# The way into attention made anew: maxima of the first heads turned into rows by TensorE, running sums put into K by VectorE, zero matmuls in early gaps

## The chip, the cores and the metric

The kernel runs on one core of one Trainium2 chip. The time is device microseconds of one execution. A core has TensorE (PE; its weight loads are listed as PEld), VectorE (DVE), ScalarE (ACT), GpSimd (POOL) and SyncE (SP, which issues nearly all DMAs here).

## What is computed

Attention for 4 batches of 8 heads, 576 positions of 64 dimensions, with a causal mask and a bias from running sums of s, and then two layers over 2304 tokens, each a product with a 512x2048 matrix, an activation and a product with a 2048x512 matrix.

```python
scores = q @ k.T / sqrt(64)
cum = cumsum(maximum(s, 0))                      # along the positions
bias = -(cum[:, None] - cum[None, :])
scores = where(causal, -1e9, scores + minimum(bias, 0))
attn = exp(scores - max(scores)); attn = attn / (sum(attn) + 1e-9)
x = attn @ v                                     # to (2304, 512)
h = x @ w_in;  x = (h - tanh(h)) @ w_out         # first layer
h = x @ w2_in; out = (h * clip(h + 3, 0, 6) / 6) @ w2_out
```

## The kernel before

**An order worked out ahead.** The kernel's functions only declare operations: `plan.op` with an engine, an estimated duration, the operations it comes after, the buffers it uses and a priority, and `plan.dma` the same for SyncE with a size. `Plan.schedule` then runs through them as a simulation, with estimated latencies (`LAT`, `DMA_US`), and the program is issued in the order of the starts that it finds. On the chip each engine goes through its own instructions in this order and waits at each for what it needs. Buffers are taken from pools; the six PSUM banks of the attention are one pool, and an operation that isn't `greedy` leaves two of them. Operations marked `port` use the SBUF port that DVE and POOL share; the planner doesn't let them overlap.

**A pair of heads.** `heads(p)` handles heads 2p and 2p+1; there are 16 pairs. q and k come as 64 rows of 576 columns a head. For products of high accuracy in a rounded type each operand is split in a high and a low part. The first pair of tiles (`firsts`, called Q and K) holds the high parts in rows 0 to 63 and four rows more: K has the running sum (high and low part, rows 64 and 65) and ones (66, 67); Q has ones (64, 65) and the negated maxima (66, 67). So the bias and the subtraction of the maximum come out of the same product. The second pair of tiles (also Q and K in the profile) holds the other combinations: `q2` copies Q's high part by DMA, `ql` and `kl` are POOL's subtractions (lines 427 and 437), `k2` a copy on ACT (433). `q1` (ACT, 421) and `kh` (DVE, 430) make the high parts of the first tiles.

**Maxima.** `mx` (line 481) multiplies the high parts for the maxima, in six matmuls a head, into `wide` and two banks; `rd` (490) reduces them on DVE with the causal mask into a column of maxima for each of five blocks of positions, `Mt`. Since the score product needs them as rows, `mf` negates and splits them (515, 516) and transposes them on DVE in blocks of 32 (519), `mo` writes them to DRAM (`mdram`) and `mi` reads them back into rows 66 and 67 of Q. Pair 0 does so head by head, the others for both heads at once.

**Scores and values.** `st` (575) makes the scores, transposed, in four chunks a head (15 matmuls, three of them the mask with an identity); `ex` (578) is the exponential on ACT, `pv` (605) the product with v in 14 matmuls, `ov` (628) the way out of PSUM.

**The start.** s is loaded for all 32 heads; DVE's `cum` clamps and scales it (371), forms running sums (372) and splits them (375, 376); a DMA puts head 0's two rows into K, and the rest goes through DRAM (`cdram`). Before it DVE fills the constant rows of head 0's Q and K and K's padding (341 to 343), and POOL those of the three other pairs of tiles, with masks and the identity.

**What comes behind.** While attention runs, twelve half blocks of the first layer's weights are read and rebuilt from two words each by ACT and DVE (`convert`, lines 748 to 779), ten more blocks afterwards. Then the first layer (830, 861) and the second (1122, 1198) follow, almost all matmuls.

Of the kernel before, what the change touches and what calls it, by code (L numbers as in the profile page):

```python
# [30 lines left out]
NW = 6  # L31
LATE_D = (7, 8, 11, 12)
# [28 lines left out]
PRIO = {  # L61
# [3 lines left out]
}  # L65
# [44 lines left out]
class Plan:  # L110
    LAT = {"PE": 0.30, "ACT": 0.05, "DVE": 0.09, "POOL": 0.09, "V": 0.0}
    DMA_US, DMA_KB_US, ISSUE = 1.6, 220.0, 0.55
# [26 lines left out]
    def schedule(self):  # L139
# [12 lines left out]
        while done < len(self.ops):  # L152
# [14 lines left out]
            while again:  # L167
                again = False
                for e in ready:
# [48 lines left out]
                    for n in o.next:  # L218
                        n.left -= 1
                        n.ready = max(n.ready, o.end)  # L220
# [18 lines left out]
def kernel(  # L239
# [87 lines left out]
    zeroed = [f32(m) for m in MTp.free] + [m.rearrange("p a i -> p (a i)") for m in mtp.free]  # L327
    s_t, c_t = (rb_t[0:NH, i * S : (i + 1) * S] for i in range(2))
    cp = [rb_t[0:NH, i * S : (i + 1) * S].bitcast(F32R) for i in (2, 3)]
# [8 lines left out]
    def prep_first(i):  # L338
        q1, k1 = firsts[i]
        eng = nc.gpsimd if i else nc.vector  # L340
        eng.memset(f32(q1)[64:68], 1.0)
        eng.memset(f32(k1)[64:68, :, 0:S], 1.0)
        eng.memset(f32(k1)[0:68, :, S:SP], 0.0)

    def prep_second():
        for _, k2 in seconds:
            nc.gpsimd.memset(f32(k2)[:, :, S:SP], 0.0)
# [17 lines left out]
    def prep_rest():  # L365
        for m in zeroed:
            nc.gpsimd.memset(m, 0.0)


    def cum():  # L370
        nc.vector.tensor_scalar(s_t, s_t, 0.0, 8.0, op0=ALU.max, op1=ALU.mult)
        nc.vector.tensor_tensor_scan(
            out=c_t, data0=c_t, data1=s_t, initial=0.0, op0=ALU.mult, op1=ALU.add
        )
        nc.vector.tensor_copy(cp[0], c_t)
        return nc.vector.tensor_sub(cp[1], c_t, f32(cp[0]))
# [944 lines left out]
```

## Time and profile before

| | |
|---|---|
| median of 3 runs | 959.87 us (958.36 to 960.94) |
| profiled execution | 957.06 us, span 955.3 us |
| mean granted TensorE clock | 0.999 |
| PE, DVE, ACT, POOL busy | 98%, 70%, 49%, 17% of the span |

The span reaches from the first to the last instruction of the profiled execution; its own time also holds what lies around it. A busy share is an average over stages with different limits. A group of instructions is named by its line, engine, operation and tiles (out<-in). In brackets behind an instruction stands how long its engine sat idle before it and what it then waited for. Matmuls overlap, so a busy PE can still run below its best rate.

### The profile page before, as it was taken

What the parts mean: (1) busy time and instruction counts of PE and PEld (TensorE: products, weight loads), DVE (VectorE), ACT (ScalarE), POOL (GpSimd) and SP (SyncE); (2) the same over time, 40 slices, a digit from 0 to 9 for tenths busy, and PEclk for the clock granted to TensorE, in tenths of its full rate; (3) what the DMA queues carried; (4) which work ended last, traced back from release to release, by engine and by line L of the source; (5) the groups of instructions that cost most, each with busy time, mean ns of one, the idle gap of its engine ahead of it and who ended that gap; (6) DMA issues with size and microseconds to landing.
All of it is one profiled execution on the core that took longest, in us unless ns stands there. A gap on an engine that the chain in (4) does not pass through costs nothing.

```text
span 955.3 us, 14956 instructions
## 1 busy us (share of the span) xinstructions
PE 933.0 (98%) x5560; PEld 831.9 (87%) x5560; DVE 672.8 (70%) x1107; ACT 464.9 (49%) x714; POOL 161.2 (17%) x106
## 2 busy tenths in 40 slices
PE   3999999999999999999999999999999999999998
PEld 3777777778878888998888888999999999999997
DVE  7887778789988766685676834657776577764763
ACT  2677677754534443444344333444454444544441
POOL 8344755600000000012222222000000000000000
PEclk9999999999999999999999999999999999999999
DMA  5667786796236448555546681776886767877672
GB/s 121 189 176 186 212 208 204 186 331 208 98 128 223 176 156 282 177 179 197 198 155 207 228 292 46 244 229 208 250 307 228 232 199 258 298 235 223 210 224 97
DMA packets 70521, 195.91 MB, mean 205 GB/s; under 512 B 11634, under 2 KB 20338, under 8 KB 69168
## 3 DMA queue, kind: packets, MB, share of 16 engines
q1 hardware_dynamic: 70448, 194.95, 64.3%
q8 instruction: 44, 0.72, 0.3%
q14 instruction: 29, 0.24, 0.1%
HBM read 143.75 MB, written 44.09 MB: 197 GB/s over the span
## 4 chain that ended last, share of the span: by engine, by line
PE 92%; DVE 3%; DMA 2%; ACT 1%; issue 1%; SPq 0%; DVEq 0%; ACTq 0%
PE bank L830 20%; PE bank L861 20%; PE pair L1198 19%; PE pair L1122 18%; PE bank L605 8%; PE bank L575 5%; DVE junk L490 1%; PE wide L481 1%; DMA tq<-in_q_dram 1%; PE bank L481 1%; DMA Q<-mdram 0%; DMA rdram<-rb 0%; ACT w L778 0%; DVE K L430 0%; DVE f_w L1142 0%
## 5 line engine op out<-in xcount | busy, mean ns | idle before, releaser
L861 PE MATMUL bank<-gg,w 128*128 128x512 f32 (+1 forms) x960 | 234.3, 368 | 0.5 <-ACT gg L849 0.3
L830 PE MATMUL bank<-xx,w 128*128 128x512 f32 (+1 forms) x960 | 233.2, 368 | 0.0
L861 PEld LDWEIGHTS bank<-gg,w 128*128 128x128 f32 x960 | 170.1, 189 | 30.9 <-ACT gg L849 1.3
L830 PEld LDWEIGHTS bank<-xx,w 128*128 128x128 f32 x960 | 170.5, 188 | 30.4
L1122 PE MATMUL pair<-op_w,w 128*128 128x384 f32 x648 | 118.0, 334 | 0.6 <-DVE f_w L1142 0.6
L841 ACT ACTIVATE g<-bank 128x512 f32<-128x512 f32 (+1 forms) x80 | 44.5, 556 | 148.2 <-PE bank L830 124.9
L1198 PE MATMUL pair<-w,op_W 128*128 128x256 f32 x918 | 115.1, 283 | 0.0
L1122 PEld LDWEIGHTS pair<-op_w,w 128*128 128x128 f32 x648 | 112.4, 188 | 1.2 <-DVE f_w L1142 0.9
L1198 PEld LDWEIGHTS pair<-w,op_W 128*128 128x128 f32 x918 | 112.8, 192 | 0.0
L605 PE MATMUL bank<-pt,vf 128*66 128x320 f32 (+4 forms) x448 | 106.9, 360 | 0.3 <-ACT pt L578 0.3
L851 POOL TENSOR_TENSOR gg<-g,gg 128x512 fp32r<-128x512 f32 x32 | 47.5, 1486 | 345.0 <-ACT gg L849 307.8
L845 DVE TENSOR_TENSOR g<-bank,g 128x512 f32<-128x512 f32 (+1 forms) x80 | 50.8, 635 | 64.4 <-ACT g L841 63.7
L575 PE MATMUL bank<-Q,K 128*128 128x320 f32 (+9 forms) x384 | 88.7, 352 | 1.6 <-ACT stage L628 1.1
L575 PEld LDWEIGHTS bank<-Q,K 128*128 128x128 f32 (+3 forms) x384 | 63.5, 186 | 23.3 <-ACT stage L628 1.7
L578 ACT ACTIVATE pt<-bank 128x512 f32<-128x512 f32 (+2 forms) x128 | 62.4, 500 | 33.3 <-PE bank L575 31.6
L849 ACT ACTIVATE gg<-g 128x512 fp32r<-128x512 f32 (+1 forms) x80 | 47.0, 587 | 43.4 <-DVE g L845 35.0
L490 DVE CUSTOM_DVE_ANT_0 junk<-bank,maskA 128x512 bf16<-128x512 f32 (+2 forms) x96 | 45.0, 469 | 20.6 <-PE bank L481 13.2
L605 PEld LDWEIGHTS bank<-pt,vf 128*66 128x66 f32 x448 | 50.5, 141 | 6.7 <-ACT pt L578 0.5
L427 POOL TENSOR_TENSOR Q<-tq,Q 64x1152 fp32r<-64x1152 f32 (+1 forms) x17 | 42.4, 2494 | 53.6 <-PE bank L575 9.0
L490 DVE CUSTOM_DVE_ANT_0 junk<-wide,maskA 128x384 bf16<-128x384 f32 x64 | 41.8, 653 | 10.0 <-PE wide L481 5.4
L437 POOL TENSOR_TENSOR K<-tq,K 64x1152 fp32r<-64x1152 f32 (+1 forms) x17 | 42.8, 2519 | 20.3 <-ACT stage L628 6.3
L1198 PE MATMUL pair<-w,op_B 128*128 128x256 f32 x342 | 44.1, 283 | 0.0
(305 smaller groups left out, 1303.3 us busy)
## 6 DMA issues: line engine op xcount, KB each, us to landing
w<-wdram SPq DMA_DIRECT2D x149, 512.0 KB
wdram<-cv SPq DMA_DIRECT2D x56, 512.0 KB
raw_c<-in_w_dram SPq DMA_DIRECT2D x11, 1024.0 KB
raw_b<-in_w_dram SPq DMA_DIRECT2D x11, 1024.0 KB
raw_a<-in_w_dram SPq DMA_DIRECT2D x12, 512.0 KB
vf<-in_v_dram SPq DMA_DIRECT2D x16, 330.0 KB
rb<-rdram SPq DMA_DIRECT2D x8, 576.0 KB
xdram<-xb SPq DMA_DIRECT2D x16, 288.0 KB
```

Source lines behind the costliest of these rows:

```text
L490: nc.vector.tensor_tensor_reduce(out=junk[0:rr, 0:w], in0=r(b)[0:rr, col : col + w], in1=maskA[0:rr, m0 : m0 + w], scale=1.0, scalar=-3.0e ...
L575: nc.tensor.matmul(o, w, x, start=(i == 0), stop=(i == len(mms) - 1), skip_group_check=True)
L578: nc.scalar.activation(r(pt), r(b)[:, 0 : CW[c]], AF.Exp, scale=0.125)
L605: nc.tensor.matmul(r(po[bank])[0:DV, oc : oc + n], r(vf)[:, j, hh, :], r(pts[c])[:, col : col + n], start=(j == 0), stop=(bank == 0 and c ...
L830: nc.tensor.matmul(r(ps)[:, 0:w], wt[:, c, :], x(c)[:, 0:w], start=(part == 0 and c == 0), stop=(part == 2 and c == NCC - 1),)
L841: nc.scalar.activation(r(g)[:, 0:w], r(ps)[:, 0:w], AF.Tanh)
L845: nc.vector.tensor_sub(x, r(ps)[:, 0:w], x)
L849: gho = plan.op("ACT", vec_us(w, 1.2, 205), lambda: nc.scalar.activation(r(gh)[:, 0:w], r(g)[:, 0:w], AF.Copy), [m, to_gg], [g, gh], base)
L851: glo = plan.op("DVE" if beside else "POOL", vec_us(w, 0.96, 155) if beside else vec_us(w, 0.44, 160), lambda: (nc.vector if beside else n ...
L861: nc.tensor.matmul(r(acc[e])[:, 0:w], a[:, es], bb[:, 0:w], start=f, stop=l)
L1122: nc.tensor.matmul(bank(k)[:, l], w[hw][:, l, kc], r(x)[:, hx, kc], start=(i in (1, 5, 2) and j == 0 and kc == 0), stop=(j == 2 and kc == ...
L1198: nc.tensor.matmul(r(c[k])[:, m * 256 : (m + 1) * 256], r(x)[:, hx, l, m * P : (m + 1) * P], w[hw][:, l], start=(i == order[chain_first[k] ...
```

## The change

Running sums: ACT clamps and scales s in place of DVE (`relu`). The sums now lie in partitions 64 to 96, with a copy of s for head 1 in partition 96 that ACT's own DMA queue loads, so that DVE can copy the high rows of heads 0 and 1 straight into K (`crow`); the low rows of these two follow by DMA. Head 0's and head 1's maxima are formed without the low row. For pair 0 ACT makes `kh`. Constant rows of pairs 1 to 3 come by DMA from those of pair 0 (`ones`), and the paddings of K are no longer filled; no product reads them.

Maxima of pairs 0 and 1 (`TURN`): instead of `mf`, `mo` and `mi` there is `turn`, twice a head (blocks 0 and 1, then 2 to 4). DVE writes the negated high and low parts beside two ones into four columns a block, PE multiplies each block by the identity, which gives four rows in PSUM, and ACT copies these into rows 64 to 67 of Q. The chunks of `mx` are taken in reverse order, so that blocks 0 and 1 are ready first, and the first chunk of scores waits only for them. The other pairs keep their way, with the negation as a subtraction from zeros and no `port` mark.

PE: ten matmuls of 512 columns on a tile of zeros at the start (`warm`), and ahead of head 1's scores zero matmuls of 256 columns wherever the planned order leaves a gap of over 0.2 us (`fill`, four fifths of the gap, 0.115 us each). They write to a bank that is held until then.

Order: all priorities are new; a table `EARLY` shifts those of the first six pairs one by one, and a table `first` orders the operations of the first six heads. Loads of q, k and v of the first pairs are tied to other operations. The planner's estimates of DMA and matmul durations change.

```diff
+TURN = (0, 1)
+WARM = 10
+EARLY = {...}
+LAG_Q = {3: 1, 4: 4, 5: 2}
+LAG_V = {1: 1, 2: 2, 3: 2, 4: 2}
+FILL_H = 1
-    DMA_US, DMA_KB_US, ISSUE = 1.6, 220.0, 0.55
+    DMA_US, DMA_KB_US, ISSUE = 1.9, 230.0, 0.62
...
-    return (4 * n / 2.4 + 6) / 1e3 if f32 else max(0.1, (n / 2.4 + (13 if n > 128 else 5)) / 1e3)
+    return (4 * n + 20) / 2.4e3 if f32 else (n + 32) / 2.4e3
...
-    s_t, c_t = (rb_t[0:NH, i * S : (i + 1) * S] for i in range(2))
+    s_t, c_t = (rb_t[D : D + NH + 1, i * S : (i + 1) * S] for i in range(2))
+    identr = att.tile([P, P], F32R, name="identr")
+    turn_t = att.tile([P, 2 * len(TURN), 5, 4], F32R, name="turn")
...
-        eng.memset(f32(k1)[0:68, :, S:SP], 0.0)
-            nc.gpsimd.memset(f32(k2)[:, :, S:SP], 0.0)
...
-        nc.vector.tensor_scalar(s_t, s_t, 0.0, 8.0, op0=ALU.max, op1=ALU.mult)
...
+    ls1 = plan.op("ACT", 0.62, lambda: nc.scalar.dma_start(s_t[NH : NH + 1], s[1:2]), prio=lead - 90, name="ls1")
+    pk0 = plan.op("POOL", 1.2, lambda: ones_k(0, nc.gpsimd), [pma], prio=lead - 39)
+    pq0 = plan.op("DVE", 1.15, lambda: ones_q(0, nc.vector), [pm0], prio=lead - 30.5)
+    sa = plan.op("ACT", 0.65, lambda: nc.scalar.activation(s_t, s_t, AF.Relu, scale=8.0), [ls, ls1], prio=lead - 30, name="relu")
+    cm = plan.op("DVE", 1.4, lambda: nc.vector.tensor_tensor_scan(
+        out=c_t, data0=c_t, data1=s_t, initial=0.0, op0=ALU.mult, op1=ALU.add), [sa, pq0], prio=lead - 29, name="cum")
+    cr = [plan.op("DVE", 0.46, lambda hh=hh: nc.vector.tensor_copy(c_row(hh, 0), c_t[NH * hh : NH * hh + 1]), [cm, pk0], prio=lead - 28 + 3 * hh, name="crow", port=True) for hh in range(2)]
...
+    cu1 = [plan.dma(lambda hh=hh: move(c_row(hh, 1), cp[1][hh : hh + 1]), 5, [cl, pk0], prio=lead - 24 + hh, name=f"cu0_lo{hh}") for hh in range(2)]
...
+    def warm():
+        for _ in range(WARM):
+            nc.tensor.matmul(r(wb)[:, 0:512], maskA[:, 0:P], maskA[:, 0:512], start=True, stop=True)
+    def fill(us):
+        for _ in range(int(us / 0.115)):
+            nc.tensor.matmul(r(wb)[:, 0:256], maskA[:, 0:P], maskA[:, 0:256], start=True, stop=True)
...
+        ones = firsts[0][1][66:68, :, 0:S]
+        def put(x):
+            move(firsts[p][x][64 + 2 * x : 66 + 2 * x, :, 0:S], ones)
+        return [plan.dma(lambda x=x: put(x), 9, [cl], prio=t, name=f"ones{p}") for x in range(2)]
...
+            def turn(hh, g):
+                i0, i1 = ((0, 2), (2, 5))[g]
...
+                    nc.vector.tensor_sub(slot[:, i0:i1, 2], none[:, 0 : i1 - i0], m)
+                    return nc.vector.scalar_tensor_tensor(
+                        out=slot[:, i0:i1, 3], in0=m, scalar=-1.0, in1=f32(slot)[:, i0:i1, 2], op0=ALU.mult, op1=ALU.subtract
+                    )
+                def rows():
+                    for i in range(i0, i1):
+                        nc.tensor.matmul(r(b)[0:4, (i - i0) * P : (i - i0 + 1) * P], slot[:, i], identr, start=(i == i0), stop=(i == i1 - 1), skip_group_check=True)
+                def put():
+                    nc.scalar.activation(r(b1)[0][64:68, hh, q0:q1], r(b)[0:4, 0 : q1 - q0], AF.Copy)
...
-            deps = [omi[x], oq2[x], ok2[x], oql[x], okl[x], pid]
+            low = [oq2[x], ok2[x], oql[x], okl[x], pmt] + (cu1 if p == 0 else [])
+            deps = [low + omi[hh][:1]] + [low + omi[hh]] * 3
...
+    filled = plan.op("V", 0.0, lambda: None, [wm, *st_done[FILL_H][:1]], [wb], prio=0, name="filled")
...
+        if o.eng == "PE":
+            if o.start < filled.start and gap and o.start - gap > 0.2:
+                fill(0.8 * (o.start - gap) - 0.1)
+            gap = o.start + o.dur
```

## Rows read from the trace of the kernel before

**Rows 1.** The page: PE's busy time, and its busy tenths in 40 slices.

```profile
PE 933.0 (98%) x5560; PEld 831.9 (87%) x5560; DVE 672.8 (70%) x1107; ACT 464.9 (49%) x714; POOL 161.2 (17%) x106
...
PE   3999999999999999999999999999999999999998
```

**Rows 2.** Windows: stretch, length, busy us per engine, granted clock, DMA share, GB/s.

```profile
0.00:20.00 20.00, 6.71 (x21) 5.32 (x21) 14.98 (x34) 6.33 (x7) 16.68 (x31) 1.00 0.42 102
20.00:40.00 20.00, 18.16 (x94) 13.71 (x93) 16.72 (x56) 10.82 (x19) 9.11 (x5) 1.00 0.70 196
60.00:100.00 40.00, 40.00 (x260) 31.68 (x259) 32.06 (x103) 30.19 (x58) 22.75 (x10) 1.00 0.73 184
20.00:200.00 180.00, 176.63 (x1110) 138.25 (x1110) 144.65 (x436) 128.32 (x244) 97.04 (x44) 1.00 0.75 197
```

**Rows 3.** Windows of line 481 alone, the maxima: PE and PEld busy.

```profile
0.00:50.00 50.00, 16.40 (x60) 11.73 (x60) 1.00 0.60 154
60.00:100.00 40.00, 9.94 (x42) 6.65 (x42) 1.00 0.73 184
```

**Rows 4.** Windows of line 575 alone, the scores: PE and PEld busy.

```profile
0.00:50.00 50.00, 11.91 (x60) 9.43 (x60) 1.00 0.60 154
60.00:100.00 40.00, 23.00 (x114) 16.50 (x115) 1.00 0.73 184
```

**Rows 5.** Timeline to the first matmul: start, us, engine, line, out<-in.

```profile
1.76 1.12 DVE L341 MEMSET Q<- 4x1280 f32 x1 [0.30 <-issue]
3.08 1.02 DVE L342 MEMSET K<- 4x1152 f32 x1 [0.19 <-issue]
...
3.96 0.68 ACT L421 ACTIVATE Q<-tq 64x576 fp32r<-64x576 f32 x1 [1.94 <-DMA tq<-in_q_dram]
...
4.25 1.12 DVE L371 TENSOR_SCALAR rb<-rb 32x576 f32<-32x576 f32 x1
5.40 1.35 DVE L372 TENSOR_TENSOR_SCAN rb<-rb 32x576 f32<-32x576 f32 x1
6.78 0.45 DVE L375 CAST rb<-rb 32x576 fp32r<-32x576 f32 x1
7.26 0.75 DVE L376 TENSOR_TENSOR rb<-rb 32x576 fp32r<-32x576 f32 x1
...
8.74 1.40 POOL L427 TENSOR_TENSOR Q<-tq,Q 64x576 fp32r<-64x576 f32 x1 [2.11 <-DVE K L430]
...
9.94 1.14 PE L481 MATMUL wide<-K,Q 66*128 66x384 f32 x3 [9.94 <-DMA K<-rb]
```

**Rows 6.** Timeline, 11 to 36 us: head 0's maxima, first scores, heads 2 and 3.

```profile
11.24 0.56 DVE L490 CUSTOM_DVE_ANT_0 junk<-wide,maskA 128x384 bf16<-128x384 f32 x1 [2.37 <-PE wide L481]
...
14.39 0.71 DVE L515 TENSOR_SCALAR MT<-Mt 128x5 fp32r<-128x5 f32 x1
...
15.57 1.13 DVE L430 CAST K<-tq 64x1152 fp32r<-64x1152 f32 x1
...
19.64 5.35 POOL L437 TENSOR_TENSOR K<-tq,K 64x576 fp32r<-64x576 f32 x3
...
22.40 0.63 PE L575 MATMUL bank<-Q,K 128*128 128x256 f32 x2
...
27.56 0.21 DVE L519 STREAM_TRANSPOSE mrow<-MT 128x32 f32<-128x32 f32 x1
...
29.31 0.38 ACT L628 ACTIVATE xb<-bank 66x256 f32<-66x256 f32 x1 [2.58 <-PE bank L605]
...
30.76 0.67 SPq L258 DMA_DIRECT2D Q<-mdram  x1
...
35.04 0.39 PE L575 MATMUL bank<-Q,K 68*128 68x256 f32 x1 [0.46 <-DMA Q<-mdram]
```

**Rows 7.** Timeline: the same three maxima matmuls (512, 256 and 128 columns), twice.

```profile
10.88 0.95 PE L481 MATMUL bank<-K,Q 66*128 66x512 f32 x3
...
28.36 0.57 PE L481 MATMUL bank<-K,Q 66*128 66x512 f32 x3
```

More of the change, by code (lines that the diff above doesn't have):

```diff
@@ L219, in schedule @@
                         n.left -= 1
-                        n.ready = max(n.ready, o.end)
+                        n.ready = max(n.ready, free[o.eng] if o.eng == n.eng != "SP" else o.end)
                         if n.left == 0:
@@ L503, in heads, with maxima @@
-        rd_done.extend(rds)
+            move(k1[64:66, :, 0:S], cdram[2 * p : 2 * p + 2].rearrange("a i s -> i a s"))
+        if p == 0:
+            ocu = [[cr[0]], [cr[1]]]
+        else:
+            ocu = [[plan.dma(cu, 5, [al, co], [b1], t0 + PRIO["cu"] + shift("cu"), name=f"cu{p}")]] * 2
         omi = []
-        for i, a in enumerate(parts):
+        def maxima(i, a):
             n = a.stop - a.start
@@ L538, in heads, with mx, rd @@
             first_mf.append(omf)
-            omi.append(plan.dma(mi, 5, [omo], [b1], u, name=f"mi{p}"))
-        lv = plan.dma(lambda: nc.sync.dma_start(r(vf).rearrange("p j a d -> p (j a d)"), v[p]), 338, first_mo[1:2] if p else first_mo[:1], [vf], t0 + PRIO["lv"], name=f"lv{p}")
+            omi.extend([[plan.dma(mi, 5, [omo], [b1], u, name=f"mi{p}")] * 2] * n)
+        mm_mx, mm_pe = {}, {}
+        for hh in range(2):
+            rds, pes = [], []
+            rows = 66 if p else 65
+            for c, tiles in enumerate(MAXT):
+                b = Buf(banks if c else widep)
+                def mx(tiles=tiles, b=b, hh=hh, rows=rows):
+                    qa, ka = (t[:, hh] for t in r(b1))
+                    for i, w, col in tiles:
+                        rr = min(P, S - i * P)
+                        cut = 512 - col if col < 512 < col + w else w
+                        for k0, n in ((0, cut), (cut, w - cut)):
+                            if not n:
+                                continue
+                            nc.tensor.matmul(
+                                r(b)[0:rr, col + k0 : col + k0 + n], qa[0:rows, i * P : i * P + rr], ka[0:rows, k0 : k0 + n],
+                                start=True, stop=True,
+                            )
+                def rd(tiles=tiles, b=b, hh=hh):
+                    for i, w, col in tiles:
+                        rr = min(P, S - i * P)
+                        m0 = 512 - i * P
+                        nc.vector.tensor_tensor_reduce(
+                            out=junk[0:rr, 0:w], in0=r(b)[0:rr, col : col + w], in1=maskA[0:rr, m0 : m0 + w],
+                            scale=1.0, scalar=-3.0e38, op0=ALU.add, op1=ALU.max,
+                            accum_out=r(mt)[0:rr, hh, i : i + 1],
+                        )
+                us = sum(mm_us(w) for _, w, _ in tiles)
+                u = t0 + hh * T + PRIO["mx"] + 0.6 * (2 - c if p in TURN else c) + shift("mx") if p else lead + 2 * hh + 0.6 * (2 - c)
+                x = min(hh, len(parts) - 1)
+                om = plan.op("PE", us, mx, [okh[x], oq1[x]] + ocu[hh], [b1, b], u, name=f"mx{2*p+hh}_{c}")
+                pes.append(om)
+                us = sum(vec_us(w, 0.96, 210) for _, w, _ in tiles)
+                rds.append(plan.op("DVE", us, rd, [om, pr, pma], [b, mt], u - PRIO["mx"] + PRIO["rd"] - shift("mx") + shift("rd") if p else u, name=f"rd{2*p+hh}_{c}"))
+            mm_mx[hh], mm_pe[hh] = rds, pes
+            if p in TURN:
+                maxima(hh, slice(hh, hh + 1))
+            elif hh:
+                maxima(0, slice(0, 2))
@@ L785 @@
             wready[fc, part] = convert(
[L786 removed]
+                fc, [part], PRIO["conv"] + 2 * fc + part, [st_done[FIRST_W][0]], rawp, wyp)
             early += wready[fc, part]
```

182 lines of the change are left out of this document (90 added, 92 removed), and 3 rows, old and new, of the table PRIO.

## Prediction

> **What bounds the kernel now.** I began with the page. Its first part gives TensorE (PE) 98% of the span, and its slices show where the other 2% lies: the first slice is three tenths busy, nearly all behind it nine [rows 1]. Next came the windows. In the first 20 us PE is busy for 6.71 us, in the next 20 for 18.16, and from 60 to 100 for all 40.00, while VectorE (DVE) has 32.06 of 40 [rows 2]. So PE sets the pace once the way in is over, and the only place with tens of microseconds to win is the way in, where PE waits.
>
> Busy time understates what the way in costs, because PE's early work runs at half speed (below) and ahead of need. I therefore count finished work by matmuls. A head has 6 maxima matmuls (line 481) and 15 score matmuls (line 575). From 60 to 100 us there are 42 and 114 [rows 3, 4], that is 7.0 heads of maxima and 7.6 of scores in 40 us. A head's maxima are 1856 columns, 0.77 us at 2.4 GHz, so 7.6 heads of scores with their values took 40 - 7.0 x 0.77 = 34.6 us, 4.55 us each. By 50 us the counts are 60 and 60 [rows 3, 4], 10 heads of maxima and 4.0 of scores: 7.7 + 18.2 = 25.9 us of work. The way in has thus lost 50 - 25.9 = 24.1 us, and this is what the change can cut.
>
> The timeline says which chain loses it. DVE fills Q and K with constants, from 4.25 clamps s (1.12), scans (1.35), splits the sum (0.45 and 0.75); a DMA carries the row into K and the first matmul starts at 9.94 [rows 5]. DVE's reduction of head 0 takes 11.24 to 14.39; then the maxima go to DRAM and back, and GpSimd (POOL) makes the low parts of K only from 19.64. The first score matmul stands at 22.40. Heads 2 and 3 are later still: their maxima are transposed at 27.77, the read back from DRAM is issued at 30.76, and PE goes on at 35.04 [rows 6].
>
> **The change part by part.**
>
> *Sums.* DVE loses the clamp (1.12) and the K fill (1.02); ACT clamps while s lands, for which it also issues a load of one row of s. s was there at 4.25 at the latest, when the clamp started; ACT's first copy, of data asked for later, starts at 3.96 [rows 5]. I put s at 3.5, the clamp on ACT at 0.65 (its 576-element copy took 0.68), the scan at 4.2 to 5.55, the copy of the row into K at 0.45 (as line 375): maxima matmuls can start at 6.1, against 9.94. ACT also makes head 0's high part of K (0.68, instead of DVE's cast); it has room, 6.33 of 20 us busy [rows 2]. The low part of the sum still travels by DMA, needed for scores alone: asked for at about 7.3 and there 2.7 us later, as from the cast's end, 7.23, to 9.94 [rows 5], so at 10.
>
> *DVE's line, head 0.* After the row copy come the splits and the second row copy (0.45 + 0.75 + 0.45), to 7.8; then the reduction, 3.15, and the new splits of the maxima, four small instructions at about 0.2, to 11.7.
>
> *Turning.* Five 128-column matmuls a head put the rows into PSUM, and ACT writes them to Q. The trace has no such group; for ACT the nearest row is the 66x256 eviction, 0.38 [rows 6]. With 0.4 for PE the rows stand in Q at 12.5. All 20 turning matmuls of four heads cost PE at least 1.1 us (128 columns each at 2.4 GHz) and at most 3.8 (0.19 each, the mean of the three matmuls that took 0.57 [rows 7]). I take 1.3, since they come in batches like those three and have fewer columns.
>
> *POOL and SyncE.* Without the memsets for pairs 1 to 3, head 0's two subtractions (1.40 each [rows 5]) follow the split sum at 6.5 and end at 9.3, hidden under the 12.5. The ones of pairs 1 to 3 become six small DMAs; SyncE issues them beside two for the sums, and no longer issues three writes and three reads of maxima. I cost that at nothing while the loads of pair 1, among which they stand, land before DVE wants them at 15.6; if not, each issue (0.67 [rows 6]) is late. v of pair 0 is now asked for at the start instead of behind the first write of maxima, well ahead of its use at 13.
>
> *First sum.* PE starts scores in earnest at 12.5 instead of 22.40, with two heads of maxima done. By the DVE line heads 1, 2, 3 follow at 15.6, 20.6, 24.5 (3.9 each, and 1.13 for K's copy [rows 6]), faster than PE consumes them, so PE is fed. Heads 4 and 5 still go through DRAM: DVE ends them at about 32.4, and from the transpose to PE's next step it was 35.04 - 27.77 = 7.3 us, giving 39.7. PE's work ahead of that ends at 12.5 + 4 x 4.55 + 4.6 (six more heads of maxima) + 1.3 = 36.6: a gap of 3 us. Work done by 39.7 is 4 x 4.55 + 8 x 0.77 = 24.4, so the way in loses 15.3 us instead of 24.1. If the read back takes 4 us, the gap goes and the loss is 36.6 - 24.4 = 12.2. The gain is 8.8 to 11.9; I take 10.
>
> *Clock and zero matmuls.* The granted clock reads 1.00 in every stretch, idle ones too [rows 2], so I go by durations: the same three matmuls took 0.95 us at 10.88, after idleness, and 0.57 at 28.36, after some six microseconds of nearly unbroken work [rows 7]. The difference, 0.38 us, is that of 896 columns at 1.2 and at 2.4 GHz. Ten zero matmuls of 512 columns run from about 1.9 to 6.2 (0.43 each at the low level) under PE's idleness; without that cover they would cost 4.3. The fillers take at most 0.8 of the gaps in the planned order; they cost nothing where a gap is real and 0.1 us each where it isn't: 0 to 1.5, I take 0.3, inside the 10. They hold one of six PSUM banks until head 1's scores, which can hold up DVE by a bank's turn, 0.7 us. The 10 counts the new scores at full speed. If zeros don't raise the clock, about 6 us of first scores run at half rate, as from 22.4 to 28.4 before, and 3 us of the gain go.
>
> The Trainium skill ("TensorE: Matmul & The Clock Gate", Part 1) says that the default state is the throttled one, that activity releases it, and that idle gaps bring it back. By its first half the sum stays; by the second a gap that the fillers miss returns the first scores to the low level, and the sum is 3 us poorer. The trace agrees with the release (0.95 to 0.57).
>
> *The rest.* Loads of later pairs are tied to other events, DVE's split of the maxima loses its mark for the port shared with POOL, and new priorities reorder the whole attention. Behind the way in PE is the bound in either order: I take 0, bounded both ways by the 3.4 us that PE idles from 20 to 200 [rows 2].
>
> **Sum.** The profiled execution took 957.06 (span 955.3 and 1.8 around it): 957.06 - 10 = 947.1. It lies 2.8 below the median shown, 959.87, and below the fastest of those three; on their scale it is 959.87 - 10 = **949.9**. A difference of 0.3% (2.9 us) is what a measurement here can tell from none.
>
> **Rivals.**
> *DVE paces the way in.* DVE is busy for 14.98 and 16.72 of the first two 20 us already [rows 2]. If its reductions start 3 us late, or heads 6 and 7 wait for DRAM as well, the gain falls to 4 to 8: 952 to 956. For it speaks the 3 us gap that I count myself; against it, two heads of maxima in stock at any time.
> *Given back later.* The attention gets 10 us shorter, but DVE's weight conversions and reductions stay: 144.65 of 180 us from 20 to 200, POOL 97.04 [rows 2]; in 170 us DVE would be 85% busy. If conversions end after the attention, the next stage waits: gain 0 to 5, 955 to 960. Against it: 25 us of DVE's time are still free.
> *The clock stays low.* Gain 7, 953. For it: nothing in the trace shows zeros raising it; against it, nor does anything tell them from other work.
> *Slower: PE stands at the turns.* PE takes matmuls in the order of the program, so a turn whose maxima are late stops the scores and values queued behind it. There are eight turns, and DVE, which makes what they wait for, is the fullest engine there. A wait of 1.25 us at each eats the 10; from 1.6 us on, 12.9 in all, the kernel is slower by over 0.3%: 963. For it speaks DVE's fullness; against it, that two turns a head are ready 1.5 us or more apart and the planner places each behind DVE's own durations.
> *It does nothing.* Hardly possible at the first matmul, 9.94, since a DMA and two DVE steps leave its chain; it is the lower end of "given back".
>
> **Chances.** Forecast (gain 8 to 13) 0.52; clock low 0.08; DVE paces 0.17; given back 0.12; slower 0.06; more than 13 (the read back quick and the 3.4 us of later idleness gone too) 0.05. Faster by over 0.3%: 0.52 + 0.08 + 0.17 + 0.05 and a third of 0.12, 0.86; within 0.3%: the rest of 0.12, 0.08; slower 0.06. The forecast's own range is 947 to 952. Leaving out the slower case, most of what is given back and the extreme of "more", the range is 943.5 to 956.
>
> **What would show it.** Right: the first line 481 matmul near 6, scores in force near 12.5, matmuls of a turn close together with little idleness ahead of them, the three 512-, 256- and 128-column matmuls at 0.57 from the start, one PE gap near 37 that ends with the DMA from mdram, and the same PE time from the end of attention to the end. Wrong: PE waiting on DVE at the turns, weight conversions that end after the last values matmul, or scores in force only after 16.

## The result: 1.25% slower instead of 1.0% faster

The changed kernel takes 970.26 us (median of 6 runs, 969.50 to 974.68), the kernel before 958.69 (6 runs beside them): a ratio of 1.0125, 95% interval 1.0104 to 1.0146. The forecast was 949.9, its range 943.5 to 956. The profiled execution took 969.5 us with a span of 967.7. Below, "after" is the changed kernel with its own line numbers: maxima 583, turning 542, scores 650, splits 535 and 536 (turned heads) and 508 and 509 (the others), GpSimd's subtractions 455 and 468.

The page of after, against [rows 1]: PE's first slice reads 8 instead of 3 (zero matmuls count as busy), but the second digit of PEclk, the granted clock in tenths, has fallen to 7.

```profile
PE 946.7 (98%) x5618; PEld 837.0 (86%) x5618; DVE 698.1 (72%) x1111; ACT 470.9 (49%) x725; POOL 154.9 (16%) x99
...
PE   8889999999999999999999999999999999999998
...
PEclk9799999999999999999999999999999999999999
```

The windows of after say where, against [rows 2].

```profile
0.00:20.00 20.00, 15.74 (x90) 9.45 (x91) 14.39 (x36) 11.54 (x18) 12.96 (x25) 1.00 0.51 140
20.00:40.00 20.00, 17.30 (x94) 13.11 (x93) 15.76 (x40) 12.10 (x24) 9.04 (x4) 0.83 0.97 235
40.00:60.00 20.00, 15.64 (x82) 12.05 (x81) 17.88 (x52) 10.52 (x18) 5.25 (x2) 0.83 0.35 91
...
20.00:200.00 180.00, 169.12 (x1034) 130.09 (x1033) 154.61 (x425) 122.19 (x229) 90.65 (x39) 0.96 0.71 182
```

From 20 to 200 us PE was busy for 176.63 us at a granted clock of 1.00 before; now it is busy for 169.12 at a mean of 0.96, and DVE has gone up by 10 us, from 144.65 to 154.61. So PE stands 7.5 us more, and part of what it does runs slower. The clock column doesn't show all of this: in before it reads 1.00 from 20 to 40 us, although the same six score matmuls took 1.79 us at first and 1.05 later, so before had a low stretch too.

```profile
22.92 1.79 PE L575 MATMUL bank<-Q,K 128*128 128x320 f32 x6
...
31.70 1.05 PE L575 MATMUL bank<-Q,K 128*128 128x320 f32 x6
```

The count of finished work that the prediction used, maxima (line 583) and scores (650) up to 50 us, against [rows 3, 4]:

```profile
0.00:50.00 50.00, 10.94 (x48) 7.26 (x48) 0.90 0.64 162
...
0.00:50.00 50.00, 11.41 (x60) 9.41 (x60) 0.90 0.64 162
```

That is 8.0 heads of maxima and 4.0 of scores, 6.2 + 18.2 = 24.4 us of work: 25.6 us lost by 50 us, where before had lost 24.1. The way in is no shorter by then. But it was: at 25 us after had finished 20 maxima and 30 score matmuls, and before had finished 24 and 11. The gain is made by 25 us and lost again by 50, and the loss goes on: the first matmul of the first layer starts at 210.25 us instead of 197.66, 12.6 later, and what lies behind it takes as long as before (967.7 - 210.25 = 757.5; 955.3 - 197.66 = 757.6).

The timeline of after shows the first place.

```profile
23.92 2.65 POOL L455 TENSOR_TENSOR Q<-tq,Q 64x1152 fp32r<-64x1152 f32 x1
23.98 0.68 DVE L592 CUSTOM_DVE_ANT_0 junk<-bank,maskA 128x512 bf16<-128x512 f32 x1
...
24.70 1.89 DVE L535 TENSOR_TENSOR turn<-none,Mt 128x3 fp32r<-128x3 f32 x1
...
26.64 2.62 POOL L468 TENSOR_TENSOR K<-tq,K 64x1152 fp32r<-64x1152 f32 x1
...
27.61 1.68 DVE L535 TENSOR_TENSOR turn<-none,Mt 128x2 fp32r<-128x2 f32 x1
...
29.63 0.28 PE L542 MATMUL bank<-identr,turn 128*4 128x128 f32 x2 [2.44 <-DVE turn L536]
...
30.14 1.80 PE L650 MATMUL bank<-Q,K 128*128 128x320 f32 x6
```

A subtraction of three columns on DVE takes 1.89 us, the next 1.68; the same instruction takes 0.17 where POOL is idle. Each ends when POOL's subtraction ends (24.70 + 1.89 = 26.59, and 23.92 + 2.65 = 26.57; 29.29 and 29.26), whereas the reduction at 23.98, which reads PSUM and one tile in SBUF, isn't touched. PE stands 2.44 us at the turn that waits for the second one, and the six score matmuls behind it take 1.80 us, where at 15.27 the same six had taken 1.05. After's granted clock is 0.51 from 30 to 35 us.

The second place, 20 us later, is where heads 4 and 5 should have come.

```profile
44.39 2.61 POOL L455 TENSOR_TENSOR Q<-tq,Q 64x1152 fp32r<-64x1152 f32 x1 [15.12 <-DVE MT L508]
44.42 2.60 DVE L509 SCALAR_TENSOR_TENSOR MT<-Mt,MT 128x10 fp32r<-128x10 f32 x1
...
47.30 0.33 SPq L262 DMA_DIRECT2D mdram<-mrow  x1
...
48.83 0.50 SPq L715 DMA_DIRECT2D xb<-stage  x1
...
49.42 0.67 SPq L262 DMA_DIRECT2D Q<-mdram  x1
...
52.65 0.67 PE L583 MATMUL wide<-K,Q 66*128 66x384 f32 x3 [2.98 <-issue]
...
53.40 0.40 PE L650 MATMUL bank<-Q,K 128*128 128x256 f32 x2
```

Their maxima go to DRAM at 47.30; the split was held for 2.43 us just before. PE runs dry for 3 us and head 4's scores start at 53.40. Before, the maxima went 10.8 us earlier, but their read back stood long in SyncE's order, so that at PE only 3.2 us are lost:

```profile
36.54 0.34 SPq L258 DMA_DIRECT2D mdram<-mrow  x1
...
45.30 0.66 SPq L258 DMA_DIRECT2D Q<-mdram  x1
...
50.19 0.64 PE L575 MATMUL bank<-Q,K 128*128 128x256 f32 x2
```

The groups of DVE's splits in after (busy us and mean ns of one):

```profile
L508 DVE TENSOR_TENSOR MT<-none,Mt 128x10 fp32r<-128x10 f32 x14 | 11.5, 823 | 0.5
L535 DVE TENSOR_TENSOR turn<-none,Mt 128x2 fp32r<-128x2 f32 (+1 forms) x8 | 5.3, 667 | 0.3
L509 DVE SCALAR_TENSOR_TENSOR MT<-Mt,MT 128x10 fp32r<-128x10 f32 x14 | 4.8, 343 | 0.5
```

Twelve of the 44 splits are held, for 16.7 us together. Before, 4 of the 17 negations were (3.6 us), in spite of their `port` mark; one of them stands in [rows 6], 0.71 us at 14.39 for what took 0.17 later. That negation reads one tile in SBUF and not two, and so does this cast of after, which takes 3.17 us beside POOL and 0.76 alone:

```profile
60.58 2.62 POOL L455 TENSOR_TENSOR Q<-tq,Q 64x1152 fp32r<-64x1152 f32 x1 [10.87 <-PE bank L650]
60.64 3.17 DVE L458 CAST K<-tq 64x1152 fp32r<-64x1152 f32 x1 [0.74 <-PE bank L650]
```

### The profile page after: what moved, and what is told of

It reads as the page before. It is cut to its first block, busy times and chain, and to the rows that moved or that the text cites. A ratio compares the mean times of both kernels' runs of the same rounds, so it can differ in the third digit from the quotient of the medians.

```text
span 967.7 us, 15051 instructions
## 1 busy us (share of the span) xinstructions
PE 946.7 (98%) x5618; PEld 837.0 (86%) x5618; DVE 698.1 (72%) x1111; ACT 470.9 (49%) x725; POOL 154.9 (16%) x99
## 4 chain that ended last, share of the span: by engine, by line
PE 91%; DVE 5%; DMA 2%; issue 1%; ACT 1%; SPq 0%; DVEq 0%; ACTq 0%
PE bank L907 20%; PE bank L938 20%; PE pair L1275 19%; PE pair L1199 18%; PE bank L680 7%; PE bank L650 5%; DVE junk L592 2%; PE wide L583 1%; DMA vf<-in_v_dram 1%; PE bank L583 1%; DMA raw_a<-in_w_dram 1%; DVE turn L535 1%; DMA tq<-in_k_dram 0%; DVE MT L508 0%; DVE K L458 0%
## 5 line engine op out<-in xcount | busy, mean ns | idle before, releaser
L938 PE MATMUL bank<-gg,w 128*128 128x512 f32 (+1 forms) x960 | 210.6, 368 | 1.4 <-ACT gg L926 1.4
L907 PE MATMUL bank<-xx,w 128*128 128x512 f32 (+1 forms) x960 | 210.1, 368 | 0.0
L1199 PEld LDWEIGHTS pair<-op_w,w 128*128 128x128 f32 x672 | 116.7, 188 | 0.1
L680 PE MATMUL bank<-pt,vf 128*66 128x320 f32 (+4 forms) x448 | 100.3, 365 | 0.0
L1275 PE MATMUL pair<-w,op_W 128*128 128x256 f32 x738 | 93.1, 283 | 0.0
L1275 PEld LDWEIGHTS pair<-w,op_W 128*128 128x128 f32 x738 | 90.7, 192 | 0.0
L650 PE MATMUL bank<-Q,K 128*128 128x320 f32 (+9 forms) x384 | 75.6, 333 | 0.3 <-ACT Q L545 0.3
L1275 PE MATMUL pair<-w,op_B 128*128 128x256 f32 x432 | 55.7, 283 | 0.0
L1275 PEld LDWEIGHTS pair<-w,op_B 128*128 128x128 f32 x432 | 53.6, 192 | 0.0
L592 DVE CUSTOM_DVE_ANT_0 junk<-bank,maskA 128x128 bf16<-128x128 f32 (+2 forms) x96 | 44.9, 467 | 10.0 <-DVE Mt L592 1.2
```

The source lines that it names most:

```text
L592: nc.vector.tensor_tensor_reduce(out=junk[0:rr, 0:w], in0=r(b)[0:rr, col : col + w], in1=maskA[0:rr, m0 : m0 + w], scale=1.0, scalar=-3.0e ...
L650: nc.tensor.matmul(o, w, x, start=(i == 0), stop=(i == len(mms) - 1), skip_group_check=True)
L680: nc.tensor.matmul(r(po[bank])[0:DV, oc : oc + n], r(vf)[:, j, hh, :], r(pts[c])[:, col : col + n], start=(j == 0), stop=(bank == 0 and c ...
L907: nc.tensor.matmul(r(ps)[:, 0:w], wt[:, c, :], x(c)[:, 0:w], start=(part == 0 and c == 0), stop=(part == 2 and c == NCC - 1),)
L938: nc.tensor.matmul(r(acc[e])[:, 0:w], a[:, es], bb[:, 0:w], start=f, stop=l)
L1199: nc.tensor.matmul(bank(k)[:, l], w[hw][:, l, kc], r(x)[:, hx, kc], start=(i in (1, 5, 2) and j == 0 and kc == 0), stop=(j == 2 and kc == ...
```

## The experiments

Each ran beside the kernel before on the same chip, so the ratio is what compares them; differences below are taken from the ratios, at 959 us for 1 (0.1% is about 1 us). Each ratio is known to 0.001 or 0.002 either way, so a difference of two to some 2 to 3 us. "Same order" means that only what is named differs: the order of each engine's work is after's. PE and clock are PE's busy time and the mean granted clock from 20 to 200 us; zero matmuls count as busy. Of 1 no trace is read; PE, clock and trace of 12 are from one more execution of that kernel, which took 962.66 us.

| kernel | us | ratio to before (95%) | PE, clock |
|---|---|---|---|
| before | 959 | | 176.63, 1.00 |
| after | 970.26 | 1.0125 (1.0104 to 1.0146) | 169.12, 0.96 |
| 1 nothing split | 966.82 | 1.0073 (1.0054 to 1.0091) | |
| 2 turned heads not split | 969.86 | 1.0112 (1.0096 to 1.0128) | 169.40, 0.94 |
| 3 the other 14 pairs not split | 966.26 | 1.0072 (1.0054 to 1.0090) | 171.82, 0.94 |
| 4 no zero matmuls | 974.63 | 1.0162 (1.0144 to 1.0180) | 169.01, 0.93 |
| 5 zero matmuls in three stands | 966.81 | 1.0081 (1.0059 to 1.0103) | 175.34, 0.97 |
| 6 = 1 + 5 | 957.62 | 0.9972 (0.9958 to 0.9986) | 178.36, 1.00 |
| 7 before, zero matmuls | 959.32 | 1.0002 (0.9987 to 1.0018) | 173.52, 0.99 |
| 8 before, nothing split | 957.97 | 0.9992 (0.9976 to 1.0008) | 173.88, 1.00 |
| 9 = 6, transposes for splits | 958.08 | 0.9982 (0.9968 to 0.9997) | 176.76, 0.99 |
| 10 = 6, read of maxima early, 17 zero matmuls fewer | 957.81 | 0.9983 (0.9969 to 0.9998) | 175.78, 0.98 |
| 11 = 10, loads early | 958.97 | 0.9999 (0.9980 to 1.0018) | 176.80, 1.00 |
| 12 = 10, bulk loads late | 963.14 | 1.0032 (1.0018 to 1.0046) | 173.66, 0.98 |
| 13 new order, nothing split | 952.65 | 0.9933 (0.9913 to 0.9952) | 179.97, 1.00 |
| 14 another order, nothing split | 952.94 | 0.9945 (0.9926 to 0.9963) | 177.07, 0.99 |
| 15 = 13, more zero matmuls | 955.96 | 0.9968 (0.9957 to 0.9978) | 179.53, 1.00 |
| 17 = 13 with the splits | 966.25 | 1.0064 (1.0044 to 1.0085) | 173.95, 0.96 |
| 18 = 13 without late zeros | 953.75 | 0.9934 (0.9911 to 0.9958) | 177.49, 1.00 |

**1 to 3: take the splits away, same order.** The reduction itself writes the negated maximum where it is wanted, so nothing is left to subtract. The low part of the maxima, the rounding rest, is zero in these kernels: scores are shifted by the rounded maximum.

```diff
                 def split():
-                    m = r(mt)[:, hh, i0:i1]
...
+                    return None
...
-                            scale=1.0, scalar=-3.0e38, op0=ALU.add, op1=ALU.max,
-                            accum_out=r(mt)[0:rr, hh, i : i + 1],
+                            scale=-1.0 if neg else 1.0, scalar=3.0e38 if neg else -3.0e38,
+                            op0=ALU.add, op1=ALU.min if neg else ALU.max, accum_out=to,
```

`neg` is true for the heads that are not split, and `to` is the place where the row is wanted. Experiment 1 does it in all pairs, 2 in the four turned heads, 3 in the other fourteen pairs.

> The changed kernel in its own order of instructions, but DVE's reductions write the negated maxima straight into the tile that is turned or transposed (the low part of the maximum is left at zero, which changes the shift of a row, not its softmax), so the two small DVE instructions that negate and split the maxima are gone in all 16 pairs. Theory A (these instructions, which read two SBUF tiles and no longer carry the port mark, stand until POOL's subtraction is over; 12 of 44 did, 16.7 us in all, and PE idles behind them and drops its clock): DVE's busy time falls by 20 us or more, PE's gap at 27 to 30 us and half of that at 50 us go, 956 to 962 us. Rival B (the new order itself, its late loads and the reductions of head 4 behind conversions, makes the loss): 967 to 970 us.

> As the run before, but for the four turned heads alone (eight splits). A: the stalls at 24.7 and 27.6 us (1.7 and 1.5 us above their normal 0.17) and the half-speed stretch behind them go, 4 to 7 us: 963 to 966. B: 969 to 971.

> As the first run, but for the 14 pairs that go through DRAM alone. A: the stalls of 2.4 us at 44.4 and of 1 to 2 us six times later go, about 11 us of DVE's time, of which PE gets back some 4 to 6: 964 to 966. B: 969 to 971.

By this held splits would be 5 of the 12 us of loss, and those of the turned heads, which the timeline blamed first, about 1, which is within the noise. Theory A had asked for more in 1 and 2; both came out near rival B. The trace of the second shows why it gained so little: PE stands as long as ever, now for ACT.

```profile
27.05 1.16 ACT L450 ACTIVATE Q<-tq 64x1152 fp32r<-64x1152 f32 x1 [1.14 <-DMA tq<-in_q_dram]
28.12 0.41 ACT L706 ACTIVATE stage<-bank 66x320 f32<-66x320 f32 x1
28.56 0.95 ACT L547 ACTIVATE Q<-bank 4x256 fp32r<-4x256 f32 x3
...
28.99 0.38 PE L653 MATMUL bank<-Q,K 68*128 68x256 f32 x1 [2.37 <-ACT Q L547]
```

The turned rows are in PSUM by 26.5, but in ACT's order their copy to Q stands behind the copy of pair 3's Q, which waits for its load, and an eviction. From 40 to 60 us the granted clock of 2 is 0.59 and that of 3 is 0.61, where after has 0.83, which takes back part of what either gains.

**4, 5 and 6: the clock, same order.** Experiment 4 issues none of the zero matmuls; 5 puts 54 more where after's trace shows PE standing; 6 is 1 and 5 together.

```diff
+        n, of = {('tr1', 3): (20, None), ('mx6_0', 1): (9, 'st3_2'), ('mx10_0', 1): (25, 'st4_0')}.get((o.name, seen[o.name]), (0, None))
+        for _ in range(n):
+            at = next(x for x in ops if x.name == of) if of else o
+            nc.tensor.matmul(at.bufs[-1].t[:, 0:256], maskA[:, 0:P], maskA[:, 0:256], start=True, stop=True)
         ins = o.fn()
```

> The changed kernel in its own order, without any zero matmul. If they raise the clock as meant, the first scores run at the low level: their three matmuls take 0.95 in place of 0.57, heads 0 and 1 end 2 to 3 us later, 971 to 973. If they only take PE's time (theory C: they stand before real matmuls), 967 to 969.

> The changed kernel, instruction order kept, with 54 more zero matmuls (256 columns, bf16) where TensorE stands in the changed kernel's trace: 20 ahead of the third turning of pair 1 (stands 27.2 to 29.6 us), 9 ahead of head 6's first maxima (41.4 to 42.5), 25 ahead of head 10's first maxima (49.7 to 52.7). Theory clock: the half-speed stretches between 29 and 60 us, which cost about 6.5 us of TensorE's time by the granted clock in the windows, follow from these stands; the clock column stays at 1.00 and the time falls by 4 to 6.5 us, to 964 to 966. Theory supply (pair 2's maxima come 10 us later than before because of the order of the work, and TensorE only waits longer if it is faster): the clock column stays high, heads 4 and 5 start within 1 us of 53.4, and the time falls by less than 1.5 us.

> The first experiment (VectorE's reduction writes the negated maxima itself, nothing is split, low parts zero, 966.8 us) with the same 54 zero matmuls in the same three places. Theory clock: 961 to 963 us, 4 to 6 us less than without them. Theory supply: 965 to 967 us. If both contention and clock were the whole of the loss, it would come to 957 us or less.

The zero matmuls of the way in are worth 3.5 us (4). Zero matmuls in the stands alone give 4.2 and nothing split alone gives 5.0; both together give 14.7, and the kernel is then a little faster than before. In 5 DVE is still held (its splits still fall under POOL's subtractions): one of them takes 2.17 us at 82.42, PE stands 1.66 us up to 86.34, where no zero matmuls are placed, and the clock from 80 to 100 is 0.83. In 6 it is 1.00 throughout:

```profile
20.00:40.00 20.00, 19.02 (x135) 14.76 (x134) 14.70 (x48) 12.64 (x24) 7.02 (x4) 1.00 1.03 248
40.00:60.00 20.00, 19.80 (x134) 15.73 (x133) 17.23 (x44) 15.26 (x27) 10.74 (x4) 1.00 0.50 125
20.00:200.00 180.00, 178.36 (x1149) 138.99 (x1148) 147.45 (x402) 126.61 (x241) 93.58 (x42) 1.00 0.75 195
```

**7 and 8: the same two cures on the kernel before.** In 7, 82 zero matmuls stand ahead of and between the first maxima; 8 changes the reduction as in 1.

```diff
+        n, of = {('mx0_0', 1): (45, None), ('mx1_0', 1): (27, 'mx1_1'), ('mx3_0', 1): (10, 'st0_0')}.get((o.name, seen[o.name]), (0, None))
```

> The kernel before with zero matmuls alone: 45 ahead of the first maxima (until 9 us), 27 in the stand at 11.8 to 15.1 us, 10 in the one at 20.1 to 21.4 us. Theory clock: head 0's scores and first products with V, which ran at half speed from 22.4 to 27.4 us, run at full speed; 2 to 3 us less, 956 to 957.5. Rival (VectorE's maxima pace the way in): within 0.5 us of before.

> The kernel before with negated maxima written by the reduction itself (two of VectorE's three instructions per pair fall away, 17 times 0.35 us, with the 3.6 us that four of them were prolonged; the low part of the maxima is left zero). Theory contention: VectorE gains up to 9 us over the attention, of which only the part before 40 us shows: 0.5 to 1.5 us less than before, 957.5 to 958.5. Rival (VectorE is never the last to be waited for in this order): within 0.5 us of before. It also says what the low parts are worth in either order.

Neither wins anything clear of the noise there. In 7 the first scores do run at full speed (the six that took 1.79 us take 1.05 at 22.58), and then PE waits for V's load and for the next maxima. In 8 DVE has 11 us less to do from 20 to 200 us (133.64 instead of 144.65), and the time is the same within its interval: in before's order PE wasn't waiting for it.

**9: is it DVE's time or the hold?** Two transposes of scratch in the place of each split.

```diff
+    def twice():
+        nc.vector.transpose(scr[0], scr[1])
+        nc.vector.transpose(scr[0], scr[1])
...
                 def split():
-                    return None
+                    twice()
```

> The sixth experiment (negated maxima written by the reduction, 54 more zero matmuls, 957.6 us) with two 32x32 transposes of scratch (0.21 us each) on VectorE in the place of every split that it left out: four for pair 0, four for pair 1, two for each of the 14 other pairs, some 7.5 us of VectorE's time, no less than the splits take when nothing holds them. Theory contention (a VectorE instruction with two inputs in SBUF stands until GpSimd's subtraction ends): the transposes are not held, each stays at 0.21 us, and the time stays under 960 us. Rival (it is VectorE's own time that counts, whatever the instruction): 964 us or more.

```profile
L434 DVE STREAM_TRANSPOSE MT<-MT 128x32 f32<-128x32 f32 x22 | 4.7, 212 | 0.8
L433 DVE STREAM_TRANSPOSE MT<-MT 128x32 f32<-128x32 f32 x22 | 4.5, 206 | 0.0
```

It is the hold. DVE has 44 more instructions, 9.2 us; 28 of them start while POOL subtracts, none takes over 0.22 us, and the time is that of 6.

**10 to 12: bring heads 4 and 5 forward by hand, order of 6 otherwise.** 10 moves the read of pair 2's maxima on SyncE directly behind their write, and head 10's first maxima behind head 4's scores; 11 also moves pair 1's loads ahead; 12 is 10 with 1.09 MB of bulk loads moved behind that read.

```diff
+    shift('mi2', 'mo2', 1)
+    shift('mx10_0', 'st4_3', 1)
+    shift('mx10_1', 'mx10_0', 1)
```

> The sixth experiment with two moves in the order and nothing else: SyncE issues pair 2's read of the turned maxima right behind their write (there it stands behind the copy of head 3's result, 2.2 us after the write has landed), and TensorE runs head 10's first maxima behind head 4's scores and not ahead of them; the 25 zero matmuls of that place are 8. Theory supply (the order gives back between 25 and 50 us what the way in gains): heads 4 and 5 start at about 45 instead of 47.25, and the time falls by 1.5 to 2.5 us, to 955 to 956. Rival (some later wait absorbs it): within 0.5 us of 957.6.

> The tenth experiment, and on SyncE pair 1's loads of Q and K ahead of the sums' low rows and the sums' copy to DRAM, the six copies of rows of ones no longer in one block ahead of pair 1's V, and head 2's first maxima on TensorE two scores and a product earlier. Theory supply: K of pair 1 is cast at about 13 us instead of 15.4, head 2's first maxima run near 17 instead of 19.2, heads 2 to 5 start 1 to 2 us earlier than in the tenth experiment, and the time is 1 to 2 us less than there. Rival (the loads only swap places in a full DMA queue): within 0.5 us of the tenth experiment, or worse because the sums' copy comes later.

> The tenth experiment with three bulk loads (Q and K of pair 6, a half slot of weights; 1.09 MB of the 5.09 MB that were moved from 20 to 45 us) behind pair 2's read of its turned maxima on SyncE; 12 zero matmuls ahead of head 4's scores. In the tenth the 16 KB write of those maxima was issued at 40.74 us and the read that waits for it only at 45.16, while the DMA engines were 98% busy up to 41 us. Theory full queue: the write lands within 2.5 us, the read is issued by 43.5, heads 4 and 5 run at about 45 instead of 47.4, and the time falls by 1.5 to 2.5 us from the tenth's 957.8, to 955.5 to 956.5. Rival (something after 50 us takes it back, as nothing but the planned order was tuned for it): within 0.7 us of 957.8.

All three missed. In 10 the write of 16 KB was issued at 40.74 us, but the read behind it only at 45.16, since the transfer stood behind bulk loads (12 shows this):

```profile
40.74 0.33 SPq L262 DMA_DIRECT2D mdram<-mrow  x1
45.16 0.67 SPq L262 DMA_DIRECT2D Q<-mdram  x1
...
47.44 0.39 PE L647 MATMUL bank<-Q,K 68*128 68x256 f32 x1 [2.34 <-DMA Q<-mdram]
```

Head 4's scores got going no earlier than in 6 (47.25), and with only 8 zero matmuls in that place PE's stand of 2.34 us was followed by a clock of 0.83 from 40 to 60 us. In 11 the load of pair 1's K is issued at 8.76 us, 2.2 earlier than in after, but K is cast at 16.31 (6: 15.36) and not at 13: in DVE's order the cast stands behind head 1's reductions, which end at 16.27 there and at 14.83 in 6. In that execution of 11 the first maxima ran at the low level (1.20 us for 0.71).

> The twelfth experiment once more, for its profile alone; it took 963.1 us, 5.3 more than the tenth. Theory full queue was wrong by then about the time; if its mechanism is right, the read of pair 2's maxima is issued by 43.5 us and the loss comes later, from the bulk loads that were put off. Rival: the write of the maxima lands as late as in the tenth (45.1).

The mechanism was right and the price was not counted: with the bulk loads moved the read is issued at 42.23, 1.75 us behind the write, and head 4's scores start at 44.93, but the half slot of weights that was put off arrives late on ACT, whose order puts it ahead of the exponentials, and PE stands 3.42 us for them, then at half speed.

```profile
40.48 0.34 SPq L262 DMA_DIRECT2D mdram<-mrow  x1
42.23 0.67 SPq L262 DMA_DIRECT2D Q<-mdram  x1
...
51.77 0.66 ACT L826 ACTIVATE wy<-raw_a 128x512 f32<-128x512 f32 x1 [7.74 <-DMA raw_a<-in_w_dram]
52.34 1.94 ACT L650 ACTIVATE pt<-bank 128x256 f32<-128x256 f32 x5
...
52.77 3.90 PE L677 MATMUL bank<-pt,vf 128*66 128x256 f32 x10 [3.42 <-ACT pt L650]
```

**13 to 15, 17 and 18: other orders.** The same planner with new numbers in `PRIO`, `EARLY`, `LAG_Q` and `LAG_V`, and durations that say that nothing is split; zero matmuls where its plan leaves PE a gap of over 0.5 us between 19 and 62 us (30 in 13).

```diff
-                o = plan.op("DVE", 0.38, split, dep, [mt], u, name=f"mf{p}")
+                o = plan.op("DVE", 0.02, split, dep, [mt], u, name=f"mf{p}")
...
-            omf = plan.op("DVE", 0.75, mf, dep, [mt, MT, mr], u, name=f"mf{p}")
+            omf = plan.op("DVE", 0.25, mf, dep, [mt, MT, mr], u, name=f"mf{p}")
```

> The first experiment's instructions (negated maxima written by the reduction) in a new order: the same planner, told that nothing is split any more (VectorE's 0.38 and 0.75 us steps gone), with other priorities; zero matmuls in the four gaps that this plan leaves on TensorE between 19 and 62 us (30 in all). It plans head 4's scores at 41.1 instead of 44.6 us. Theory supply (once VectorE is not held and the clock stays up, what is missing from the forecast is that pair 2 comes late): heads 4 and 5 start near 43.5 instead of 47.25 (sixth experiment), and the time is 953 to 956. Rival (no order gets pair 2 through the DRAM round trip early enough to matter, or each gap in the new order drops the clock again): 957 to 962.

> As the thirteenth experiment, with another set of priorities (head 4's scores planned at 40.7 us) and 23 zero matmuls in three gaps. Theory supply: 953 to 956. Rival: 957 to 962. Two orders tell whether a gain or a loss belongs to the supply of pair 2 or to one lucky order.

> The thirteenth experiment's order with 67 zero matmuls instead of 30 in the same four places. Theory clock: if the thirteenth shows stretches at half speed between 20 and 60 us, this one doesn't, and is 1 to 4 us faster. Rival (there the clock holds already): the same time within 0.5 us, or up to 2 us more because the zero matmuls stand in front of work that is ready.

> The thirteenth experiment's order (952.65 us) with the change's own splits of the maxima put back (subtraction and scaled subtraction on VectorE, low parts filled), as the plan has no time for them. Theory contention: a split of these is held until GpSimd's subtraction ends (up to 2.6 us) wherever the two meet; in the change's order that cost 9.2 us when the clock was kept up (966.8 against 957.6); here 5 to 10 us, 958 to 963. Rival (the good order has slack for it, the holds hurt only the change's tight order): under 955 us.

> The thirteenth experiment without its 30 zero matmuls between 19 and 62 us (those of the way in up to 19 us stay). Theory clock: the gaps that they fill, 0.7 to 1.2 us each in the plan, drop the clock to half for some microseconds, 2 to 4 us more: 954.5 to 957. Rival (such short gaps don't lower the clock, and without zero matmuls TensorE takes ready work sooner): 952 to 953.

In 13 pair 2's maxima go out at 36.91 us, head 4's scores start at 41.49 (after 53.40, experiment 6 47.25), and PE has no gap left:

```profile
13.00 1.01 PE L647 MATMUL bank<-Q,K 128*128 128x320 f32 x6
...
41.49 0.49 PE L647 MATMUL bank<-Q,K 128*128 128x256 f32 x2
...
20.00:200.00 180.00, 179.97 (x1139) 139.59 (x1138) 144.69 (x404) 126.69 (x243) 94.17 (x42) 1.00 0.75 202
```

It is 0.7% faster than before, and 14 says that this isn't one lucky order. More zero matmuls only stand in front of ready work (15, 3.4 us worse); without any after 19 us nothing is lost by the ratio (18: stands of up to 0.87 us, clock 1.00). With the splits back in that order, 17 is as slow as after's order without them. Its trace has the whole chain in one place:

```profile
9.61 2.76 POOL L455 TENSOR_TENSOR Q<-tq,Q 64x576 fp32r<-64x576 f32 x2 [0.40 <-DVE K L391]
...
10.43 0.60 DVE L535 TENSOR_TENSOR turn<-none,Mt 128x2 fp32r<-128x2 f32 x1
11.06 1.32 DVE L536 SCALAR_TENSOR_TENSOR turn<-Mt,turn 128x2 fp32r<-128x2 f32 x1
...
12.53 0.37 PE L542 MATMUL bank<-identr,turn 128*4 128x128 f32 x2 [1.93 <-DVE turn L536]
...
16.43 1.75 PE L650 MATMUL bank<-Q,K 128*128 128x320 f32 x6
```

Two small splits are held, each until one of POOL's two subtractions ends (the second at 12.37), 1.6 us in all. PE stands 1.93 us at the first turn, the clock is 0.50 from 13 to 22 us, and six score matmuls take 1.75 us instead of 1.01: 13 had begun them at 13.00, 17 at 16.43. By the first scores of head 1 (18.54 and 24.52) 17 is 6.0 us behind.

## Why the prediction was wrong

*The step that failed: "DVE's split of the maxima loses its mark for the port shared with POOL", costed at nothing under "The rest".* Before, the negation carried the mark, so the planner kept POOL's marked work off it. After, the split is a subtraction and a scaled subtraction of two tiles in SBUF, without the mark, so the plan puts them under POOL's subtractions. Splits replaced by other instructions (9) and splits put back (17) show that held splits cost this time: 12.5 us in a good order (13 to 17), and in after's order 10.5 where zero matmuls keep the clock up (5 to 6) and 5.0 where they don't (after to 1). In 17 the splits' own time on DVE, some 7 us, is not separated from the hold; in after's order 9 separates it and finds nothing. That the lost mark brings them together is read from the planner, not shown by a run: with the mark 4 of 17 were held before, and taking them away there won nothing (8). The bound of 3.4 us that I set was PE's idleness in the kernel before; it bounds what a new order can win and says nothing of what it can lose. The row that should have warned is in [rows 6]: 0.71 us for a five-column instruction.

The Trainium skill ("GPSIMD Engine Reference", section Specifications) says that GpSimd's way into SBUF is shared with VectorE and that there is contention with VectorE instructions that run in a 2-port mode or have two inputs in SBUF. The trace agrees, and shows the length: not a slower instruction but a split that ends when GpSimd's ends (26.59 and 26.57). The negations of before and the cast of K at 60.64 were held with one input; in which mode they ran no trace shows.

*The clock: right for the way in, wrong behind it.* Zero matmuls do raise it (three maxima matmuls into `wide` take 0.71 us at 13.10, where they took 1.14 at 9.94 before [rows 5]; experiment 4 costs 3.5). But "the 10 counts the new scores at full speed" held only up to the first stand that no zero matmul covers, 27.2 to 29.6 us; 20 to 60 us ran at 0.83. I had written down the rule that idleness brings the low level back, and priced it for the first scores alone, at 3 us.

*Heads 4 and 5: 39.7 us forecast, 53.40 measured (before: 50.19).* I took DVE to be through with them at 32.4, as if it went from one head to the next (and left out pair 2's copy of K, 1.13 us; with it my own terms give 33.4). After's DVE stands 2.57 us before head 2's reduction, behind head 1's scores in PE's order, is held for 3.5 at pair 1's splits, and reaches head 4 at 37.76. With no split held and the clock up it is still 47.25 (6), so the rest, 7.5 us, belongs to the order itself; in 13 it is 41.49.

*What was right.* The way in: first maxima at 6.84 (6.1 forecast; a table load of 1.28 us stands ahead of ACT's clamp), head 0's rows in Q at 14.84 and scores in force from 15.27 (both 12.5 forecast, so 2.3 and 2.8 late). Most of this lateness is the hold again: POOL's first subtractions are done in time, but two of head 0's splits stand under them (1.28 us at 9.66 and 0.70 at 13.08), and in the same order scores are in force at 13.17 with nothing split (6) and at 13.74 with transposes in the splits' place (9). The turning takes eight groups of 0.28 to 0.42 us, 2.6 instead of 1.3. Behind the attention nothing changes.

*The rivals.* "Slower: PE stands at the turns" named the place and the engine waited for, but asked for 1.6 us at each of eight turns. PE stood 3.3 us at the turns in all, 2.44 of it at one, and unsplit turns alone won about 1 us (2); the rest lies with the clock and the splits of the other pairs. "DVE paces" may be what remains in 6, which no run shows. "Given back later" did not happen; it was given back at once.

*The sum.* 22 us lie between the forecast's -10 and the measured +12. Holds and clock are 14.7 of them (after to 6), the order 3.7 (6 to 13); the last 3.6 (13 gains 6.4 and not 10) stay open. Late first scores don't explain them, since in 13 these are in force at 13.00, half a microsecond late. By 50 us 13 has finished 48 maxima and 90 score matmuls, 33.5 us of work, so it has lost 16.5 where a gain of 10 needed 14.1. Putting the mark back was not tried by itself: it makes the planner choose another order.

## What to carry to other kernels

When an instruction on DVE loses what kept it apart from GpSimd's, ask whom it can now collide with: even one of two columns waits for the rest of a long GpSimd instruction, and if TensorE's next matmul hangs on it, 1.6 us become 6 (17 against 13). Two cures that give 5 and 4 us alone can give 15 together, so a cause isn't refuted by a single cure that does little. And an order planned to the last gap is worth only as much as the durations in it: look first for what the plan doesn't model, and give the plan that.

## What the runs showed of the hardware

- A DVE instruction with two inputs in SBUF and two to ten columns took 0.17 us alone and up to 2.60 beside a GpSimd subtraction; the ends agree within 0.03 us. With one input from SBUF, a negation of ten columns took up to 1.43 us (before, at 98.67) and a cast of K 3.17 instead of 0.76. Reductions from PSUM with one SBUF tile and 32x32 transposes (44 of them, 28 started inside a GpSimd subtraction, at most 0.22 us) were not held.
- TensorE's granted clock fell to 0.51 after a stand of 2.44 us (after, 30 to 35 us) and to 0.50 behind one of 1.07 (after, up to 42.46; 44 to 47 us), and stayed low for several microseconds of busy work; in 18, with stands of up to 0.87 us, it read 1.00 from 20 to 200 us.
- Where a read waits for a write of 16 KB and stands right behind it in SyncE's order, its issue came 1.75 us after that of the write with bulk loads moved away (12: 40.48 to 42.23), and 4.4 us behind them (10: 40.74 to 45.16).
